# Whole float32 softmax parts for six half pairs, more transposes by DMA, float32 cluster similarities

## The chip, the core and the metric

One core of a Trainium2 chip runs the whole kernel. The metric is the device time of one execution in microseconds (us). The engines are TensorE (PE, its weight loads apart as PEld), VectorE (DVE), ScalarE (ACT), GpSimd (POOL) and SyncE (SP, which issues most DMAs). Each works through its own instructions in order and waits for others by semaphores.

## What is computed

A clustered attention and two feed-forward blocks. A query attends only to the keys whose nearest centroid is its own.

```python
B, H, S, D = 2, 8, 768, 64            # 16 heads in all, 16 centroids a head
q_assign = argmax(q_n @ c_n, axis=-1)  # normalised; the same for keys
mask = q_assign[:, :, :, None] == k_assign[:, :, None, :]
scores = where(mask, q @ k.T / sqrt(D), -1e9)
attn = exp(scores - max(scores)); attn /= sum(attn) + 1e-9
x = (attn @ v), heads side by side     # 1536 tokens x 512
h = x @ w_in;  x = elu(h) @ w_out      # 512 -> 2048 -> 512
out = ((x @ w_a) * (x @ w_b)) @ w_out2 # 512 -> 1536 -> 512
```

## The kernel before

Every step is a small function marked `@op`, and the string `ORDER` lists all steps as words such as `sc:3.4` (score tile 4 of head 3). The loop at the end calls them in that order; so each engine gets its instructions in the order of the words that use it, and tile pools add the waits. The 60 words `wm` are groups of eight bfloat16 products that go nowhere and stand between the early steps. An index after the last dot often names the engine (0 DVE, 1 ACT, 2 POOL).

Heads go in pairs, 8 pairs `j` of heads 2j and 2j+1; the 768 queries of a head are 6 tiles `t` of 128, in two halves `f` of three tiles.

- Loads: `lk` brings a head's transposed keys (64x768), `lq` its transposed queries twice, one copy under the other. `qa`, `qb`, `ka1`, `ka2`, `kb`/`kbd` split scaled queries and keys into a rounded part and its rest (`kbd` copies by DMA).
- Similarities: `sm` (two halves per pair) sums eight products of split centroids (`cst`, made by `c4`) with the split queries and keys, 64x384, in PSUM; `sv` copies them out; `st` transposes six blocks back to tokens by centroids (`tp`). `m1` to `m5` find the maximum's place and make a one-hot matrix, `oh`, `ohs`, `ohd` turn it and put it as 16 rows into `qb` and `kb`, so that the mask comes with the score product. For pair 0 `ot` and `oe` do this.
- Scores: `sc` makes a tile 128x768 in PSUM with four products (two buffers), `rm` takes its negative maximum on DVE, `ex` the exponential `pf` and its sum on ACT.
- Softmax parts for the value product need keys on partitions. Of the 96 tiles 66 go over PE: `tr` transposes three blocks of float32 `pf` into PSUM, `th` rounds them to float16 (first part), and `tl` on DVE subtracts that from PSUM to give the second part. Each is called twice per tile. The other 30 go by DMA: `hi` rounds `pf` to float16, `lo` on POOL subtracts to give the rest, and `td` issues one DMA transpose of both parts from SP's queue.
- Values: `vl` loads them into `acc`, `vs` scales them per head (`staged`), `v1` and `v2` split them into two float16 parts. `av` (three words per pair and half) adds six key blocks x three products of parts, for each of two heads, which write different halves of the output partitions.
- Scaling: `ra`, `rc` invert the sums, `rx` spreads them on POOL, `rb` turns them with three products with the identity, `re` copies them out and `ev` multiplies the value product by them into `acc`.
- Feed-forward weights come as 64-bit numbers in 68 pieces; `wl` loads a piece, `wa` to `wq` split it. The first pieces are made during attention.

Of the kernel before, what the change touches and what calls it, by code (L numbers as in the profile page):

```python
# [10 lines left out]
F32 = mybir.dt.float32  # L11
F32R = mybir.dt.float32r
F16 = mybir.dt.float16
# [28 lines left out]
NPHL = 3  # L42
# [35 lines left out]
rm:0.3 ex:1.2 wm:44 tl:1.0.1 w2:1 lq:5.0 tr:1.0.0 wm:12 th:1.0.0.1 v1:1.1 tr:1.1.0 th:1.1.0.1 sc:0.4
wm:9 tl:1.0.0 wm:36 rm:0.4 ra:0.0 ex:0.3 w3:1 w4:1 rc:0.0 tr:1.1.1 lk:4.0 th:1.1.1.1 sm:1.1 sc:0.5
hi:1.2.1 tl:1.1.1 ex:0.4 sv:1.1.1 wm:34 st:1 tl:1.1.0 rm:0.5 qa:4.1 wm:32 kbd:2 lo:1.2 ka1:4.2  # L80
v1:2.1 wh:1 ex:0.5 td:0.2 tr:0.3.0 sc:1.4 wm:35 rx:0.0 tr:0.3.1 sc:1.3 lk:5.0 th:0.3.0.1 m1:1
hi:0.5.1 m2:1 th:0.3.1.1 v2:1.2 v2:2.2 m3:1 m4:1 ka2:4.2 m5:1 tl:0.3.0 wm:43 oh:1 rm:1.3 ohs:1
tr:0.4.0 ex:1.3 tl:0.3.1 rm:1.4 ws:1 qb:4 th:0.4.0.1 td:1.2 av:0.0.0 rb:0.0 ohd:1 tr:0.4.1 sc:1.5
re:0.0.1 th:0.4.1.1 wl:2 tl:0.4.0 rm:1.5 tl:0.4.1 ex:1.4 qa:5.1 wq:1 tr:1.3.0 th:1.3.0.1 tr:1.3.1
av:0.0.1 th:1.3.1.0 tr:1.4.1 lq:7.0 ex:1.5 th:1.4.1.1 lo:0.5 ra:0.1 tl:1.3.1 sc:2.0 tl:1.3.0 rm:2.0
hi:1.5.1 tr:1.4.0 sc:2.1 ex:2.0 av:0.0.2 ka1:5.2 vs:4 lo:1.5 td:0.5 tl:1.4.1 rm:2.1 sc:2.2 tr:2.0.0
th:1.4.0.1 rc:0.1 tr:2.0.1 tl:1.4.0 ex:2.1 th:2.0.0.1 th:2.0.1.1 rx:0.1 lk:6.0 sc:3.0 rm:2.2 ex:2.2
rb:0.1 td:1.5 tl:2.0.0 tl:2.0.1 ka2:5.2 qb:5 rm:3.0 tr:2.1.1 ev:0.0 hi:2.2.2 sc:3.1 re:0.1.1
tr:2.1.0 wa:2 lo:2.2 sm:2.0 th:2.1.0.1 lq:6.0 ex:3.0 lk:7.0 sc:3.2 rm:3.1 sv:2.0.1 tr:3.0.0
th:2.1.1.1 ex:3.1 tl:2.1.0 w0:2 w1:2 sm:2.1 th:3.0.0.1 rm:3.2 tl:2.1.1 tl:3.0.0 ex:3.2 ra:1.0  # L90
tr:3.1.0 w2:2 sv:2.1.1 sc:2.3 rc:1.0 w3:2 th:3.1.0.1 tr:3.0.1 sc:2.4 av:0.1.0 rm:2.3 st:2 tl:3.1.0
th:3.0.1.1 rx:1.0 hi:3.2.1 ex:2.3 w4:2 tl:3.0.1 m1:2 m2:2 wh:2 tr:3.1.1 lo:3.2 rm:2.4 sc:2.5 wl:3
ws:2 m3:2 rm:2.5 v1:3.1 qa:6.1 rb:1.0 re:1.0.1 av:0.1.1 th:3.1.1.1 m4:2 ka1:6.2 av:0.1.2 m5:2
tl:3.1.1 ex:2.4 tr:2.3.0 sc:3.3 oh:2 tr:2.3.1 ex:2.5 ka2:6.2 th:2.3.0.1 td:3.2 wq:2 ohs:2 kbd:4
v2:3.2 sc:3.4 td:2.2 rm:3.3 tr:2.4.1 tl:2.3.0 ev:0.1 ex:3.3 hi:2.5.2 th:2.3.1.1 th:2.4.1.1 tr:2.4.0
rm:3.4 lo:2.5 sc:3.5 ex:3.4 th:2.4.0.1 tl:2.3.1 av:1.0.0 rm:3.5 av:1.0.1 wa:3 qa:7.1 av:1.0.2 ohd:2
ka1:7.1 ex:3.5 tl:2.4.1 qb:6 qb:7 ka2:7.2 sc:4.0 tr:3.3.0 tr:3.4.1 th:3.3.0.1 kbd:5 tl:2.4.0 sc:4.1
tr:3.3.1 hi:3.5.1 rm:4.0 tl:3.3.0 w0:3 th:3.4.1.1 rm:4.1 ex:4.0 lq:9.0 lo:3.5 tl:3.4.1 vs:5
th:3.3.1.1 ra:1.1 rc:1.1 ex:4.1 tl:3.3.1 w1:3 rx:1.1 sm:3.0 sc:4.2 tr:3.4.0 sv:3.0.1 tr:4.0.0 sc:5.0
th:3.4.0.1 rm:4.2 v1:4.2 rb:1.1 th:4.0.0.1 vs:7 tl:3.4.0 ex:4.2 re:1.1.1 tr:4.1.0 hi:4.2.1 sc:5.1  # L100
tl:4.0.0 tr:4.0.1 w2:3 sm:3.1 lo:4.2 vs:6 th:4.1.0.1 rm:5.0 th:4.0.1.1 lq:8.0 ex:5.0 v1:5.2 tl:4.1.0
# [1039 lines left out]
```

## Time and profile before

| | us |
|---|---|
| median of 3 runs | 818.26 (817.41 to 818.92) |
| profiled execution | 818.15 |
| its span, first to last instruction | 816.4 |

| engine | busy us of the span | instructions |
|---|---|---|
| PE | 807.5 | 4626 |
| DVE | 592.6 | 876 |
| ACT | 410.8 | 737 |
| POOL | 340.7 | 295 |

A group of instructions is shown with its line, engine, operation, out<-in, count, then busy time, mean duration of one in ns, and the idle time before them. Records of consecutive PE instructions overlap, since an instruction enters while the one before it drains; so a PE instruction is priced by how far apart the starts are, not by the mean duration.

### The profile page before, as it was taken

Reading aid. Unit: us, or ns where it says so; the run is one execution under the profiler, and the core shown is the slowest. Engines: PE = TensorE matmul, PEld = TensorE weight load, DVE = VectorE, ACT = ScalarE, POOL = GpSimd, SP = SyncE. Lnnn points to the kernel's source line nnn. Section 1 sums busy time; section 2 is a strip of 40 time slices with the busy share of each in tenths; the row PEclk is TensorE's granted clock in tenths of the full one; section 3 lists DMA queues with packets and bytes.
Section 4 is the critical chain, followed back from the end, with each engine's and each line's share of the span. In section 5 each row is a group of like instructions: output and inputs, shape, how many; then the busy total and the mean of one; then the engine's idle time right before and its main releaser. Section 6 shows DMA issues by size and latency. Waiting matters only on the chain.

```text
span 816.4 us, 12164 instructions
## 1 busy us (share of the span) xinstructions
PE 807.5 (99%) x4626; PEld 655.4 (80%) x4626; DVE 592.6 (73%) x876; ACT 410.8 (50%) x737; POOL 340.7 (42%) x295
## 2 busy tenths in 40 slices
PE   9999999999999999999999999999999999999998
PEld 8877777777777888888888888888888888888886
DVE  5889898999999757898778787875257874565222
ACT  7689878888896542643544464432122322232020
POOL 3576786587462233464444442341043441422000
PEclk9999999999999999999999999999999999999999
DMA  9446655565542202232222212122002221110102
GB/s 278 110 97 129 146 125 110 129 138 116 110 81 78 78 27 78 77 104 78 79 95 81 80 60 72 52 77 78 1 26 77 78 78 52 53 52 0 52 1 103
DMA packets 65626, 68.12 MB, mean 83 GB/s; under 512 B 49888, under 2 KB 49888, under 8 KB 65568
## 3 DMA queue, kind: packets, MB, share of 16 engines
q1 hardware_dynamic: 65328, 66.76, 30.6%
q8 instruction: 36, 0.59, 0.3%
q10 hardware_dynamic: 240, 0.59, 0.3%
q14 instruction: 22, 0.18, 0.1%
HBM read 48.27 MB, written 3.15 MB: 63 GB/s over the span
## 4 chain that ended last, share of the span: by engine, by line
PE 90%; POOL 5%; ACT 3%; issue 2%; DVE 0%; POOLq 0%; ACTq 0%
PE ab L927 8%; PE ab L925 8%; PE ab L926 8%; PE sc L673 6%; PE h L926 5%; PE h L925 5%; PE x L926 5%; PE x L925 5%; PE h L927 5%; PE x L927 5%; PE av L786 4%; PE o L927 4%; PE o L925 4%; PE o L926 4%; PE tt L727 4%; PE warm_ps L409 3%
## 5 line engine op out<-in xcount | busy, mean ns | idle before, releaser
L681 DVE TENSOR_REDUCE nm<-sc 128x1 f32<-128x768 f32 x96 | 90.8, 950 | 7.1 <-PE sc L673 6.0
L694 ACT ACTIVATE pf<-sc,nm 128x768 f32<-128x768 f32 x96 | 86.8, 905 | 15.7 <-POOL phl L709 6.9
L1027 ACT COPY t0ab<-ab 128x512 f32<-128x512 f32 x36 | 21.1, 587 | 108.5 <-PE ab L927 108.5
L736 DVE TENSOR_TENSOR pt<-tt,pt 128x384 f16<-128x384 f32 x132 | 70.0, 545 | 5.0 <-ACT pt L731 4.6
L1032 DVE TENSOR_TENSOR t1ab<-ab,t0ab 128x512 f32<-128x512 f32 x36 | 24.8, 688 | 63.2 <-ACT t0ab L1027 63.2
L727 PE MATMUL tt<-identf,pf 128*128 128x128 f32 x396 | 62.0, 277 | 1.4 <-ACT pf L694 1.4
L731 ACT CAST pt<-tt 128x384 f16<-128x384 f32 x122 | 55.9, 478 | 10.4 <-PE tt L727 9.8
L709 POOL TENSOR_TENSOR phl<-pf,phl 128x768 f16<-128x768 f32 x30 | 50.0, 1668 | 24.8 <-ACT phl L702 23.5
L673 PE MATMUL sc<-ka,qa 128*128 128x384 f32 x192 | 57.6, 381 | 2.5 <-ACT pf L694 2.4
L856 ACT ACTIVATE wg<-wraw 128x512 f32<-128x512 f32 x68 | 45.1, 667 | 25.5 <-DMA wraw<-in_w_out_dram 13.8
L727 PEld LDWEIGHTS tt<-identf,pf 128*128 128x128 f32 x396 | 46.0, 140 | 12.0 <-issue 4.3
L786 PE MATMUL av<-pt,v 128*64 128x384 f16 x576 | 52.7, 329 | 0.0
L873 DVE SCALAR_TENSOR_TENSOR wf<-wraw,wg 128x512 int32<-128x512 int32 x68 | 51.0, 751 | 1.8
L886 DVE SCALAR_TENSOR_TENSOR wg<-wraw,wg 128x512 f32<-128x512 uint32 x68 | 49.1, 723 | 1.7
L673 PE MATMUL sc<-kb,qb 80*128 80x384 f32 x192 | 49.6, 339 | 0.0
L1043 DVE TENSOR_TENSOR gl<-t1ab,gh 128x512 fp32r<-128x512 f32 x36 | 33.9, 941 | 18.7 <-ACT gh L1038 18.5
L861 DVE TENSOR_SCALAR wg<-wg 128x512 f32<-128x512 f32 x68 | 38.4, 566 | 8.8 <-ACT wg L856 8.6
L786 PEld LDWEIGHTS <-v 128*64 128x64 f16 x576 | 30.0, 109 | 18.4 <-issue 7.1
L866 DVE TENSOR_SCALAR wg<-wg 128x512 int32<-128x512 int32 x68 | 38.5, 567 | 1.8
L989 ACT CAST gh<-t1h 128x1024 fp32r<-128x1024 f32 x24 | 25.3, 1052 | 27.7 <-DVE t1h L981 27.7
L1083 DVE TENSOR_TENSOR acc<-o,acc 128x1024 f32<-128x1024 f32 (+1 forms) x12 | 14.2, 1180 | 32.3 <-PE o L927 32.3
L971 ACT ACTIVATE t0h<-h 128x1024 f32<-128x1024 f32 x24 | 24.6, 1024 | 23.3 <-PE h L927 23.2
(386 smaller groups left out, 2349.6 us busy)
## 6 DMA issues: line engine op xcount, KB each, us to landing
wraw<-in_w_out_dram SPq DMA_DIRECT2D x28, 512.0 KB, 3.3
wraw<-in_w_in_dram SPq DMA_DIRECT2D x16, 512.0 KB, 3.6
wraw<-in_w_a_dram SPq DMA_DIRECT2D x12, 512.0 KB, 3.5
wraw<-in_w_b_dram SPq DMA_DIRECT2D x12, 512.0 KB, 3.4
rawq<-in_qt_dram SPq DMA_DIRECT2D x30, 192.0 KB, 3.6
acc<-in_v_dram SPq DMA_DIRECT2D x4, 768.0 KB, 11.0
rawk<-in_kt_dram SPq DMA_DIRECT2D x15, 192.0 KB, 3.7
kb<-ka SPq DMA_DIRECT2D x14, 192.0 KB, 3.7
```

The lines of the kernel that those rows point to most:

```text
L673: nc.tensor.matmul(s[:, j, :HALF], a[:, qs], b[:, j * HALF : (j + 1) * HALF], start=i == 0, stop=i == 1,)
L681: nc.vector.reduce_max(out=nm, in_=st[g][f"sc{t}"][:, :, :HALF], axis=AX.XY, negate=True)
L694: nc.scalar.activation(pf.rearrange("p (a b) -> p a b", a=2), st[g].pop(f"sc{t}")[:, :, :HALF], AF.Exp, bias=st[g].pop(f"nm{t}"), accum_ou ...
L709: nc.gpsimd.tensor_sub(phl[:, S:], st[g].pop(f"pf{t}"), phl[:, :S])
L727: nc.tensor.transpose(tt[:, k * P : (k + 1) * P], pf[:, o : o + P], identf)
L731: (nc.vector.tensor_copy, nc.scalar.copy)[e](next(parts_of(g, t, u)), st[g][f"tt{t}{u}"])
L736: nc.vector.tensor_sub(lo, st[g].pop(f"tt{t}{u}"), hi)
L786: nc.tensor.matmul(pairs[j]["av"][x * 64 : (x + 1) * 64].rearrange("p (a q) -> p a q", a=3), st[2 * j + x][("v1", "v2")[vi]][:, kt_, :], s ...
L873: nc.vector.scalar_tensor_tensor(out=f, in0=raws[n][:, :, 1], scalar=-0x40000000, in1=g, op0=ALU.bitwise_and, op1=ALU.bitwise_or,)
L925: nc.tensor.matmul(ps, lhi, rhi, start=first, stop=False)
L926: nc.tensor.matmul(ps, lhi, rlo, start=False, stop=False)
L927: nc.tensor.matmul(ps, llo, rhi, start=False, stop=last)
```

## The change

- Similarities: `lk` loads the keys of both heads of a pair (128x768), a new `lp` does the same for queries, beside `lq`, which stays. `sm` is one step per pair: for each of six token blocks it multiplies the raw 128x128 block of queries, then of keys, as weights with 32 columns of normalised centroids (`cblk`, both heads' blocks) in plain float32, straight into `tp`. `sv` and `st` and the split centroids go. In odd heads the key parts now lie in swapped partition halves (`halves`).
- Whole parts: for the six (pair, half) in `WHOLE`, the first halves of pairs 0 to 5, `tr` works as before, `th` copies in float32 (no `tl`), and a new `aw` multiplies these with the unsplit `staged` values in float32. Of the other tiles, 54 go by `td` and six over PE with `tl`.
- `rb` uses transposes in place of products with the identity.
- Engines: `lo`, `qb`, `ka2` can run on DVE. Of 54 `lo` 19 stand on DVE and 35 on POOL; of 54 `hi` 38 on ACT; of 84 `th` 27 on DVE.
- `phl` has four buffers, not three, and a word in `ORDER` can name the buffer it takes. `ORDER` is another list throughout. `ce`, which loads the exponential's table early, moves to the end of attention.

Words that differ in number: `tr` and `th` 132 to 84, `tl` 132 to 12, `hi`, `lo`, `td` 30 to 54, `av` 48 to 30, `aw` 0 to 18, `sm` 16 to 8, `sv` 16 to 0, `st` 8 to 0, `lk` 16 to 8, `lp` 0 to 8.

```diff
-NPHL = 3
+NPHL = 4
+
+WHOLE = {(0, 0), (1, 0), (2, 0), (3, 0), (4, 0), (5, 0)}
...
     @op
-    def sm(j, hf):
...
-        for n, (a, b) in enumerate(prods):
-            nc.tensor.matmul(ps, a, b, start=n == 0, stop=n == len(prods) - 1)
...
+    def sm(j):
         tp = pairs[j]["tp"] = small([P, NT, 64], f"tp_{j}")
+        c = cblk[:, j % (H // 2)].rearrange("p x c -> p (x c)")
         for t in range(NT):
-            nc.tensor.transpose(
-                tp[:, t, :], pairs[j]["sim"][:, t * P : (t + 1) * P], identf[:64, :64]
-            )
+            for n, name in enumerate(("rawp", "rawk")):
+                nc.tensor.matmul(
+                    tp[:, t, 32 * n : 32 * n + 32], pairs[j][name][:, t * P : (t + 1) * P], c,
+                    start=True, stop=True,
+                )
...
     @op
-    def lo(g, t):
+    def lo(g, t, e):
         phl = st[g][f"phl{t}"]
-        nc.gpsimd.tensor_sub(phl[:, S:], st[g].pop(f"pf{t}"), phl[:, :S])
+        (nc.vector, None, nc.gpsimd)[e].tensor_sub(phl[:, S:], st[g].pop(f"pf{t}"), phl[:, :S])
 
     def pt_of(g, f):
         if f"pt{f}" not in st[g]:
-            st[g][f"pt{f}"] = take(ap, "pt", [P, 3, 2 * NT, P], F16, f"pt{f}_{g}", 4)
+            shape, dt = ([P, 3, NT, P], F32) if (g // 2, f) in WHOLE else ([P, 3, 2 * NT, P], F16)
+            st[g][f"pt{f}"] = take(ap, "pt", shape, dt, f"pt{f}_{g}", 4)
         return st[g][f"pt{f}"]
...
         for a in range(3):
-            nc.tensor.matmul(p[:, a, :], pairs[j]["rx", f][:, a, :], identf, start=True, stop=True)
+            nc.tensor.transpose(p[:, a, :], pairs[j]["rx", f][:, a, :], identf)
...
+    def aw(j, f, n):
+        if n == 0:
+            pairs[j]["av"] = take(psumA, "av", [P, HALF], F32, f"av_{j}_{f}")
+        for kt_ in (2 * n, 2 * n + 1):
+            for x in range(2):
+                g = 2 * j + x
+                nc.tensor.matmul(
+                    pairs[j]["av"][x * 64 : (x + 1) * 64].rearrange("p (a q) -> p a q", a=3),
+                    staged(g)[:, kt_ * D : (kt_ + 1) * D], st[g][f"pt{f}"][:, :, kt_, :],
+                    start=kt_ == 0, stop=kt_ == NT - 1,
+                )
```

## Rows read from the trace of the kernel before

**Rows 1.** The page: busy time in us, then tenths in 40 slices.

```profile
PE 807.5 (99%) x4626; PEld 655.4 (80%) x4626; DVE 592.6 (73%) x876; ACT 410.8 (50%) x737; POOL 340.7 (42%) x295
...
DVE  5889898999999757898778787875257874565222
...
PEclk9999999999999999999999999999999999999999
```

**Rows 2.** Stretches: length, busy PE, PEld, DVE, ACT, POOL, clock, DMA share, GB/s.

```profile
30.30:269.80 239.50, 235.42 (x1823) 180.07 (x1821) 219.93 (x367) 198.80 (x421) 149.36 (x135) 1.00 0.52 113
269.80:816.40 546.60, 542.94 (x2396) 449.23 (x2394) 355.28 (x472) 191.11 (x268) 177.56 (x122) 1.00 0.20 63
```

**Rows 3.** The chain in order of time: start us, us, engine, tile, line, count.

```profile
1.20 14.36 PE warm_ps L409 x216
...
124.50 1.82 PE sm L573 x8
126.32 0.91 PE sc L673 x4
127.23 0.99 PE tt L727 x9
...
128.92 0.82 PE rbp L767 x6
129.74 0.52 PE tp L587 x6
...
132.50 2.07 PE av L786 x24
```

**Rows 4.** Groups of DVE by form: `tl`, `th`, `re`; columns as on the page.

```profile
L736 DVE TENSOR_TENSOR pt<-tt,pt 128x384 f16<-128x384 f32 x132 | 70.0, 545 | 5.0 <-ACT pt L731 4.6
...
L731 DVE CAST pt<-tt 128x384 f16<-128x384 f32 x10 | 5.5, 548 | 2.3 <-PE tt L727 2.3
...
L772 DVE COPY rb<-rbp 128x384 f32<-128x384 f32 x4 | 2.2, 554 | 0.5 <-PE rbp L767 0.4
```

**Rows 5.** Groups of ACT by form: `th`, `hi`, `sv`, `ka1`.

```profile
L731 ACT CAST pt<-tt 128x384 f16<-128x384 f32 x122 | 55.9, 478 | 10.4 <-PE tt L727 9.8
...
L702 ACT CAST phl<-pf 128x768 f16<-128x768 f32 x12 | 10.0, 837 | 0.0
...
L579 ACT COPY sim<-sm 64x384 f32<-64x384 f32 x12 | 5.6, 464 | 1.3 <-PE sm L573 1.2
...
L523 ACT CAST ka<-rawk 64x768 fp32r<-64x768 f32 x6 | 4.9, 830 | 0.1
```

**Rows 6.** Single lines: subtractions in SBUF on DVE, shortest/median/longest ns, first and last start.

```profile
L944 DVE TENSOR_TENSOR x1l<-acc,x1h x4: 1211/1220/1227, 254.1 to 510.5; 128x1024 fp32r<-128x1024 f32 x4
...
L530 DVE TENSOR_TENSOR ka<-rawk,ka x1: 1946/1946/1946, 6.6 to 6.6; 64x768 fp32r<-64x768 f32 x1
...
L1043 DVE TENSOR_TENSOR gl<-t1ab,gh x36: 677/694/1781, 526.5 to 793.1; 128x512 fp32r<-128x512 f32 x36
```

**Rows 7.** DMA transposes: issues and landing; a pair of them on SP; stretches as in Rows 2.

```profile
L741 SPq DMA_TRANSPOSE pt<-phl x30: 1275/1440/2931, 42.1 to 241.7; - x30
...
DMA to landing us min/median/max: 3.6/3.8/5.5
...
92.02 3.71 SPq L741 DMA_TRANSPOSE pt<-phl  x2
...
60.00:240.00 180.00, 176.76 (x1336) 134.04 (x1337) 166.84 (x277) 155.89 (x338) 121.58 (x110) 1.00 0.58 123
94.00:98.00 4.00, 4.00 (x28) 3.49 (x27) 3.74 (x8) 3.77 (x11) 3.10 (x5) 1.00 1.09 196
98.00:100.00 2.00, 2.00 (x12) 1.35 (x12) 1.71 (x4) 2.00 (x5) 1.09 (x1) 1.00 0.18 71
```

**Rows 8.** Timeline: the first score product on PE; the exponential's table load on ACT.

```profile
30.35 0.60 PE L673 MATMUL sc<-ka,qa 128*128 128x384 f32 x2
...
9.72 1.28 ACT L346 ACT_TABLE_LOAD   x1
```

More of the change, by code (lines that the diff above doesn't have):

```diff
@@ L299, in clustered_attention_moe_kernel @@
     pools = {}
+    named, taken = {}, {}
     def take(pool, tag, shape, dt, name, bufs=1):
-        return pool.tile(shape, dt, tag=tag, bufs=bufs, name=name)
+        if bufs > 1:
+            n = taken[tag] = int(named.pop(tag, (taken.get(tag, -1) + 1) % bufs))
+            tag = f"{tag}_{n}"
+        return pool.tile(shape, dt, tag=tag, bufs=1, name=name)
     def small(shape, name, dt=F32):
@@ L355, in cz @@
     def cz(_):
-        for k in ("q1", "q2", "k1", "k2"):
-            nc.gpsimd.memset(cst[k].bitcast(F32), 0.0)
+        nc.gpsimd.memset(cblk, 0.0)
     @op
@@ L481, in flat, with minus_scaled @@
         return t.rearrange("p t d -> p (t d)")
-    def minus_scaled(out, a, scale, b):
-        nc.vector.scalar_tensor_tensor(
+    def minus_scaled(e, out, a, scale, b):
+        (nc.vector, None, nc.gpsimd)[e].scalar_tensor_tensor(
             out=out, in0=a, scalar=scale, in1=b, op0=ALU.mult, op1=ALU.subtract
@@ L503, in lk, with lp @@
     @op
-    def lk(g, e):
-        t = st[g]["rawk"] = take(ep, "rawk", [64, S], F32, f"rawk_{g}", 2)
-        (nc.sync, nc.scalar)[e].dma_start(out=t, in_=kt[g])
+    def lk(j, e):
+        t = pairs[j]["rawk"] = take(ep, "rawk", [P, S], F32, f"rawk_{j}", 2)
+        (nc.sync, nc.scalar)[e].dma_start(out=t, in_=kt[2 * j : 2 * j + 2].rearrange("x d s -> (x d) s"))
+    @op
+    def lp(j, e):
+        t = pairs[j]["rawp"] = take(ep, "rawp", [P, S], F32, f"rawp_{j}", 2)
+        (nc.sync, nc.scalar)[e].dma_start(out=t, in_=qt[2 * j : 2 * j + 2].rearrange("x d s -> (x d) s"))
     @op
@@ L519, in operand, with halves @@
         return st[g][name]
+    def halves(g):
+        x = 64 * (g % 2)
+        return slice(x, x + 64), slice(64 - x, P - x)
     @op
     def ka1(g, e):
+        a, _ = halves(g)
         (nc.vector.tensor_copy, nc.scalar.copy, nc.gpsimd.tensor_copy)[e](
-            operand(g, "ka")[0:64], st[g]["rawk"]
+            operand(g, "ka")[a], pairs[g // 2]["rawk"][a]
         )
@@ L528, in ka2 @@
     def ka2(g, e):
-        k = operand(g, "ka")
-        (nc.vector, None, nc.gpsimd)[e].tensor_sub(k[64:P], st[g]["rawk"], k[0:64].bitcast(F32))
+        k, (a, b) = operand(g, "ka"), halves(g)
+        (nc.vector, None, nc.gpsimd)[e].tensor_sub(
+            k[b], pairs[g // 2]["rawk"][a], k[a].bitcast(F32)
+        )
     @op
     def kb(g):
-        nc.scalar.copy(operand(g, "kb")[0:64], st[g]["rawk"])
+        nc.scalar.copy(operand(g, "kb")[0:64], pairs[g // 2]["rawk"][halves(g)[0]])
     @op
@@ L538, in kbd @@
         nc.sync.dma_start(
-            out=operand(g, "kb")[0:64].bitcast(F32), in_=operand(g, "ka")[0:64].bitcast(F32)
+            out=operand(g, "kb")[0:64].bitcast(F32),
+            in_=operand(g, "ka")[halves(g)[0]].bitcast(F32),
         )
@@ L717, in parts_of @@
         f, a = divmod(t, 3)
-        return (pt_of(g, f)[:, a, i * NT + 3 * u : i * NT + 3 * (u + 1)].rearrange("p m q -> p (m q)")
-                for i in range(2))
+        parts = 1 if (g // 2, f) in WHOLE else 2
+        return [pt_of(g, f)[:, a, i * NT + 3 * u : i * NT + 3 * (u + 1)].rearrange("p m q -> p (m q)")
+                for i in range(parts)]
     @op
@@ L1092, in ob @@
         send(a, t)
-    for word in ORDER.split():
+    for line in ORDER.split():
+        word, *buffers = line.split("/")
+        named.update(n.split("=") for n in buffers)
         name, args = word.split(":")
```

443 lines of the change are left out of this document (218 added, 225 removed).

## The prediction

> **What bounds the kernel now.** I read the page first, then stretches of busy time, then the chain of waits in order of time, then single lines. [rows 1] TensorE (PE) is busy for 807.5 of 816.4 us, at the full granted clock in all forty slices. A busy PE alone proves little, so the reader looks at the two stretches of [rows 2]: from the first score product (30.35 us [rows 8]) to the last scaling of attention (269.8 us) PE is busy for 235.4 of 239.5 us, VectorE (DVE) for 219.9 (92%), ScalarE (ACT) for 198.8 (83%), GpSimd (POOL) for 149.4. Behind that, in the feed-forward part, PE is full again and the others have room. [rows 3] shows the same as a chain: from 124.50 to 134.57 us nearly every piece is PE, one behind the other. So time is what PE has to do, and an edit is worth its PE time so long as DVE, ACT and the DMAs keep up, and DVE has 20 us to spare in the stretch, no more.
>
> **PE, part by part**, priced by the contiguous pieces of [rows 3]. A similarity product costs 1.82/8 = 0.228 us, a transpose of a similarity block 0.52/6 = 0.087, a softmax transpose 0.99/9 = 0.110, an instruction of the float32 product that spreads the reciprocals 0.82/6 = 0.137 (three products, six records: a float32 product is two instructions), a value product in float16 2.07/24 = 0.086, a warm-up product in bfloat16 14.36/216 = 0.066.
>
> *Similarities.* Gone: 8 pairs x 16 products = 128 x 0.228 = 29.2 us, and 48 transposes x 0.087 = 4.2. Added: 8 x 12 float32 products = 192 instructions that load 128 weight columns and pass only 32. No row has this form. The nearest is the transpose of a similarity block (float32, 128 weight columns, 64 passed): 0.087. From above the reciprocal's 0.137 (128 passed) bounds it, from below the warm-up's 0.066. I take 0.075, under the nearest row since half as many columns pass: 14.4 us (12.7 to 26.3). Net -19.0 (-7 to -21).
>
> A page speaks against this. The Trainium skill, "TensorE: Matmul & The Clock Gate", LDWEIGHTS (loading the stationary operand), counts 1/1.2 ns per weight column whatever the rows, 107 ns for 128. By it the 192 instructions would take an estimated 20.5 us and the kernel would end about 6 us later than my sum. The trace disagrees: the similarity transposes load 128 columns each and follow each other at 87 ns [rows 3].
>
> *Reciprocals.* 96 instructions x 0.137 = 13.1 become 48 transposes x 0.110 = 5.3: -7.8.
>
> *Softmax transposes.* 132 groups of three become 84: 144 x 0.110 = -15.8. (36 tiles of the whole halves and 6 of the last pair stay on PE; 54 instead of 30 go by DMA.)
>
> *Value products.* Six halves lose 36 float16 products each: 216 x 0.086 = -18.6. They get 12 float32 products each, 144 instructions of 384 columns. Here I chose. Two float16 products into different output halves run side by side: 0.086 each, where a score product of the same 384 columns takes 0.91/4 = 0.228. A float32 instruction takes twice a bfloat16 one of the same shape (0.137 against 0.066). If float32 pairs run side by side too, one costs 2 x 0.086 = 0.172, in all 24.8 us; if not, twice that, 49.5. Both instructions of one product write the same half, so only every second neighbour can overlap, which in a row of them still keeps both halves busy. I take 24.8: net +6.2 (end: +31).
>
> Sum: -19.0 - 7.8 - 15.8 + 6.2 = -36.4 us of PE work. Warm-ups are as many as before (60 groups), so nothing is bought there. Some 3 us of it fall ahead of the first score product (one pair's similarities shrink and three groups of warm-ups move behind it); the stretch would shrink from 239.5 to about 206.
>
> **Who must keep up in 206 us.** *DVE* [rows 4, 6]: 120 of 132 subtractions go (70.0/132 = 0.530): -63.6; three similarity evictions (0.55, as the other copies from PSUM) -1.6; 17 more casts from PSUM (0.55) +9.4; four more evictions of reciprocals (0.55) +2.2; six small operations on the values' scale move behind the first score product, +2.4. New are 19 subtractions of 128x768 in SBUF and four more of 64x768. 1024 elements a partition take 1.21 us undisturbed, so 768 take 0.91; but the one 64x768 that DVE did took 1.95, with POOL at work, and the 128x512 ones spread from 0.68 to 1.78. I take 1.2 each, +27.6 (0.91 to 1.95: 21 to 45). DVE: 219.9 - 23.6 = 196. *ACT* [rows 5]: 65 casts less (55.9/122 = 0.458) -29.8, 12 similarity evictions less (5.6/12 = 0.47) -5.6, 4 reciprocal evictions less -1.9; 26 more float16 casts (0.83) +21.7, 5 key casts (0.82) +4.1. One table load of 1.28 [rows 8] no longer sits behind the warm-ups but in front of the first exponential. Some 189. *POOL* loses more key work than it gains in subtractions and stays near 146; I cost that at nothing, covered by a third of the stretch free.
>
> So DVE would be wanted for 196 of 206 us, 95%. An in-order engine is not on time at that share: I let the stretch grow until DVE is back at the 92% at which PE ran without gaps before, 196/0.92 = 213. That gives back 7 us. ACT then stands at 89%, up from 83.
>
> *DMA and SP's queue* [rows 7]. Before, the DMA engines were 58% busy from 60 to 240 us: 104 us. Two transposes behind each other (92.02) filled the engines at 1.09 for about 4 us, so one is worth at most 2.2. 24 more are 52 us, the queries' second load (3.1 MB; 123 GB/s at 58% is 212 at full) 15. That makes 171 us of 1.09-wide engine time in some 170 us: about 92% full. SP issues them in order at 1.44 each, 78 us for 54; key and query loads, copies of keys and one-hot rows stand behind a transpose that waits for its subtraction, and PE's next scores and value products wait for those. I put no time of its own on this, since the pieces overlap DVE's lag, but it is the thinnest cover.
>
> **Result of the likeliest case.** Profiled execution 818.15 us, 1.75 of it around the span, 0.1 below the median of 818.26. 818.15 - 36.4 + 7 = 789 (780 to 797 with 0.066 to 0.1 for a similarity instruction and 0 to 14 us of lag).
>
> **Rivals.** *B: float32 value products don't run side by side.* 24.8 more on PE; the others then have room again and the lag goes: 818.15 - 36.4 + 24.8 = 806 (801 to 809). For it: no row shows a float32 pair; against: the float16 pair.
>
> *C: DVE or the transposes set the pace.* If each of the 23 SBUF subtractions costs 1.95, DVE has 213 us to do and at 92% the stretch is 232: 7 us gained there, 3 ahead of it, 808; with a share of 95%, 224, 800. Full DMA engines (171 us at 92% of their 1.09, in bursts) end in the same place. So 798 to 812. For it: the long ones of [rows 6]; against: most of these operations are short ones.
>
> The page for this is the Trainium skill, "SBUF — State Buffer", SBUF: two separate sides: a VectorE operation with two SBUF inputs and a GpSimd operation shut each other out for a whole instruction. The trace agrees in part: of 128x512 subtractions the median is 694 ns, the longest 1781 [rows 6].
>
> *D: slower: transposes one at a time.* If a transpose must land (3.8 us) before the next moves, 54 of them take 205. They start near 55 us and the last was followed by 28 us of work (241.7 to 269.8): 55 + 205 + 28 = 288, 18 us later than before, 836. It decides from (269.8 - 28 - 55)/54 = 3.5 us a transpose. Against it: the two at 92.02 are issued within 3.71 us and done by 98, where the DMA share falls to 0.18.
>
> *E: no change*, savings all eaten by lag: 818.
>
> **How the numbers follow.** Forecast 0.55, B 0.14, C 0.17, D 0.07, E 0.03, and 0.04 for under 779 (no lag at all, similarities at the low end). The range 778 to 811 holds the first three, about 0.84, and takes in the bounds of the similarity and the value products. Faster by over 0.2% (what a measurement tells from no change, 1.6 us): 0.55 + 0.14 + 0.17 + 0.04 = 0.90; within 0.03; slower 0.07.
>
> **What would show it.** Similarity instructions closer than 0.09 us; value products in float32 near 0.17 us an instruction (0.34 is B); last scaling near 240 us instead of 269.8 with PE pieces still filling the chain; DVE near 92% of that stretch, its SBUF subtractions between 0.91 and 1.3 us (1.9 is C); SP's transposes issued near 1.5 us, DMA share under 1. The feed-forward part should keep its 546.6 us to within 2. I am wrong if PE shows idle time of more than some 15 us in the stretch, or if the feed-forward part starts short of weights.

## The result and the profile after

The changed kernel takes 811.24 us (810.02 to 812.25) beside 817.84 us for the kernel before on the same chip: 0.9917 of it, interval 0.9899 to 0.9935, a gain of 6.6 us. The forecast of 789 was a gain of 29, and 811.24 lies just above the upper end of 811. The profiled execution took 810.02 us, its span is 808.2. A trace shows one execution, here the shortest of four, so differences between traces can be some us off those between medians.

The page (busy time, tenths in 40 slices; against [rows 1]):

```profile
PE 789.1 (98%) x4378; PEld 642.4 (79%) x4378; DVE 576.4 (71%) x792; ACT 405.4 (50%) x689; POOL 339.1 (42%) x284
...
DVE  4899888889888867898777697875257873565222
...
PEclk9999998999899999999999999999999999999999
DMA  9558994989991212223222321122011221110102
```

Stretches, columns as in [rows 2]: first score product to last scaling, the feed-forward part, and two pieces of the first; under them the last piece in the kernel before:

```profile
28.40:260.50 232.10, 218.97 (x1580) 166.82 (x1578) 206.20 (x291) 192.44 (x374) 154.21 (x131) 0.97 0.80 165
260.50:808.20 547.70, 544.11 (x2400) 450.18 (x2399) 357.34 (x473) 192.93 (x270) 177.72 (x122) 1.00 0.20 63
...
130.00:165.00 35.00, 34.31 (x249) 24.97 (x248) 31.66 (x45) 31.15 (x60) 26.68 (x23) 1.00 0.78 157
...
195.00:245.00 50.00, 42.32 (x289) 29.06 (x286) 44.44 (x60) 42.20 (x81) 30.40 (x26) 0.93 1.04 190
```

```profile
195.00:245.00 50.00, 49.47 (x389) 38.57 (x388) 47.31 (x78) 44.40 (x99) 30.11 (x27) 1.00 0.48 91
```

Against [rows 2] the stretch shrank from 239.5 to 232.1 us, where 206 to 213 were forecast; the feed-forward part kept its time (547.7 against 546.6). PE is now idle for 13.1 us of the stretch (4.1 before) and its clock is down to 0.97 of full. From 195 to 245 us it is idle for 7.7 us (0.5 before) while DVE and ACT are at 89 and 84%: PE doesn't bound that piece any more.

The time between the start of one PE instruction and the start of the next, summed by kind over the attention's instructions (worked out from the two traces), shows where the sum went:

```
us on PE by kind                       before   after   change  forecast
similarities (products, transposes)     36.25   21.50   -14.75    -19.0
reciprocals                             11.49    6.89    -4.60     -7.8
softmax transposes                      42.59   31.70   -10.89    -15.8
value products                          51.66   62.60   +10.94     +6.2
score products                          79.20   88.67    +9.47      0
warm-ups, one-hot rows, others          34.66   36.42    +1.76      0
sum                                    255.85  247.78    -8.1     -36.4
of it: beyond 300 ns to the next start    4.1    20.3   +16.2
of it: the rest (PE's own pace)         251.7   227.5   -24.2
```

So the 28 us that are missing from PE's sum are of two kinds: 12 in its own pace, and 16 of waits, of which the forecast had allowed 7. PE's own pace also holds what its lower clock costs. Of the 20.3 us of waits 11.0 stand ahead of score products, which take a score buffer that the exponential must leave. What the weight load of score products waits for, before and then after (line, releaser, us, times, longest):

```profile
PEld sc L673 <- ACT pf L694: 5.6, 11, 1.1
```

```profile
PEld sc L683 <- ACT pf L704: 18.7, 30, 1.9
```

When they arise is seen in the starts of the score products, tile by tile (96 tiles in order of time; us from the span's start, worked out from the traces; the columns from "half tr." on are experiments below):

```
tile      before   after  half tr.  6 buf.  no lo   least   lo twice
0          30.35   28.35   28.14    28.14   28.24   28.02    28.12
16         67.55   64.82   64.54    63.92   62.99   63.42    66.44
40        127.97  114.81  114.11   113.52  112.52  112.31   121.91
44        135.83  130.09  128.20   124.45  122.46  122.25   133.10
64        179.18  173.05  171.12   168.22  164.39  164.08   178.14
80        218.56  208.47  205.72   203.30  198.96  196.95   223.91
95        249.70  239.02  237.06   234.76  228.30  226.34   263.62
last sc.  270.43  261.12  259.12   256.87  250.37  248.12   285.71
```

("last sc." is the end of the last scaling.) After has a lead of 13.2 us at tile 40, which is near the pace of the forecast. It loses 7.4 of it within four tiles, and ends with 9.3. Of the 7.4 us 2.1 are work that its order has there: "least" takes 9.94 us for these four tiles with PE never waiting and at full clock, before took 7.86. The other 5.3 us are waits (2.5) and a slower pace at a mean clock of 0.78. The four tiles stand in the chain of waits (start us, us, engine, tile, line; the first row is the same work elsewhere):

```profile
66.11 2.60 PE tp L596 x24
...
112.10 1.44 PE av L812 x8
...
114.53 3.28 DVE qb L502
...
118.33 3.44 PE tp L596 x24
```

on GpSimd and PE at that place (timeline):

```profile
114.43 1.78 POOL L519 TENSOR_TENSOR v<-acc,v 128x384 f16<-128x384 f32 x2
116.18 0.82 POOL L509 TENSOR_TENSOR acc<-acc,vsc 128x384 f32<-128x384 f32 x1
...
118.33 0.41 PE L596 MATMUL tp<-cblk,rawp 128*128 128x32 f32 x2 [1.91 <-DVE pt L743]
```

and the stretch behind it, with the clock:

```profile
120.00:124.00 4.00, 4.00 (x21) 3.90 (x21) 1.93 (x5) 2.38 (x6) 3.51 (x2) 0.55 0.28 86
```

A `qb` operation of DVE takes 3.28 us at 114.53; the same operation took 0.94 at its shortest in this kernel and 1.12 at its longest before. It ends 0.81 us after the last of three GpSimd operations that ran meanwhile, nearly the whole of its own shortest time. PE waits 1.91 us behind it, its clock then stands at 0.55 for four us, most of them at the lower of its two levels (1.2 rather than 2.4 GHz), and 24 similarity instructions take 3.44 us, where the 24 at 66.11 took 2.60.

### The profile page after: what moved, and what is told of

Its sections match the earlier page's. It is cut to its first block, busy times and chain, and to the rows that moved or that the text cites. A ratio compares the mean times of both kernels' runs of the same rounds, so it can differ in the third digit from the quotient of the medians.

```text
span 808.2 us, 11612 instructions
## 1 busy us (share of the span) xinstructions
PE 789.1 (98%) x4378; PEld 642.4 (79%) x4378; DVE 576.4 (71%) x792; ACT 405.4 (50%) x689; POOL 339.1 (42%) x284
## 4 chain that ended last, share of the span: by engine, by line
PE 83%; DMA 5%; DVE 5%; ACT 4%; issue 2%; POOL 1%; SPq 0%; ACTq 0%; DVEq 0%; POOLq 0%
PE ab L951 8%; PE ab L952 8%; PE ab L950 8%; PE h L950 5%; PE h L952 5%; PE x L950 5%; PE x L952 5%; PE h L951 5%; PE x L951 5%; PE sc L683 5%; PE o L951 4%; PE o L952 4%; PE o L950 4%; PE av L798 3%; DMA pt<-phl 2%; PE tt L739 2%
## 5 line engine op out<-in xcount | busy, mean ns | idle before, releaser
L691 DVE TENSOR_REDUCE nm<-sc 128x1 f32<-128x768 f32 x96 | 90.6, 951 | 14.4 <-PE sc L683 13.4
L719 POOL TENSOR_TENSOR phl<-pf,phl 128x768 f16<-128x768 f32 x35 | 60.3, 1725 | 28.1 <-ACT phl L712 25.5
L1057 DVE TENSOR_TENSOR t1ab<-ab,t0ab 128x512 f32<-128x512 f32 x36 | 24.8, 689 | 63.2 <-ACT t0ab L1052 63.2
L683 PE MATMUL sc<-ka,qa 128*128 128x384 f32 x192 | 59.6, 392 | 8.5 <-ACT pf L704 7.3
L881 ACT ACTIVATE wg<-wraw 128x512 f32<-128x512 f32 x68 | 45.3, 672 | 24.8 <-DMA wraw<-in_w_out_dram 15.3
L898 DVE SCALAR_TENSOR_TENSOR wf<-wraw,wg 128x512 int32<-128x512 int32 x68 | 52.7, 775 | 1.8
L683 PEld LDWEIGHTS sc<-ka,qa 128*128 128x128 f32 x192 | 30.1, 196 | 23.3 <-ACT pf L704 18.7
L739 PE MATMUL tt<-identf,pf 128*128 128x128 f32 x252 | 40.6, 283 | 1.0 <-ACT pf L704 0.8
L1021 DVE TENSOR_TENSOR gl<-t1h,gh 128x1024 fp32r<-128x1024 f32 x24 | 31.9, 1331 | 8.7 <-ACT gh L1014 8.7
L739 PEld LDWEIGHTS tt<-identf,pf 128*128 128x128 f32 x252 | 30.6, 145 | 8.3 <-ACT pf L704 3.6
L1006 DVE SCALAR_TENSOR_TENSOR t1h<-t0h,h 128x1024 f32<-128x1024 f32 x24 | 29.1, 1216 | 10.6 <-ACT t0h L1001 10.6
L683 PEld LDWEIGHTS sc<-kb,qb 80*128 80x128 f32 x192 | 36.2, 195 | 0.0
```

The costliest lines, as they stand in the source:

```text
L683: nc.tensor.matmul(s[:, j, :HALF], a[:, qs], b[:, j * HALF : (j + 1) * HALF], start=i == 0, stop=i == 1,)
L691: nc.vector.reduce_max(out=nm, in_=st[g][f"sc{t}"][:, :, :HALF], axis=AX.XY, negate=True)
L719: (nc.vector, None, nc.gpsimd)[e].tensor_sub(phl[:, S:], st[g].pop(f"pf{t}"), phl[:, :S])
L739: nc.tensor.transpose(tt[:, k * P : (k + 1) * P], pf[:, o : o + P], identf)
L881: nc.scalar.activation(wgf[n][0].bitcast(F32), raws[n][:, :, 1].bitcast(F32), AF.Abs)
L898: nc.vector.scalar_tensor_tensor(out=f, in0=raws[n][:, :, 1], scalar=-0x40000000, in1=g, op0=ALU.bitwise_and, op1=ALU.bitwise_or,)
```

## Experiments

Four theories were set against each other at first. Theory 1: the DMA engines are full. Theory 2: four buffers for softmax parts are too few, so casts wait for transposes. Theory 3: DVE's operations on two SBUF inputs and GpSimd's shut each other out. Theory 4: it is PE's own work, similarity instructions above all. A fifth came from the first runs.

**Half of each transpose.**

```
-        nc.sync.dma_start_transpose(out=pt_of(g, f)[:, a], in_=...)
+        nc.sync.dma_start_transpose(out=pt_of(g, f)[:, a, :NT], in_=...[:, :S])
...
-                    st[2 * j + x][f"pt{f}"][:, :, pi * NT + kt_, :],
+                    st[2 * j + x][f"pt{f}"][:, :, kt_, :],
```

> The changed kernel, but each of the 54 DMA transposes moves only the first float16 part (768 of 1536 columns), and the value products read that part where they should read the second; so the second part of the softmax is left out there. Nothing else moves. Theory 1 (the DMA engines are full: share 1.08 from 195 to 243 us, and PE waits behind it): the share there falls under 0.8, PE's idle time in attention from about 18 us to under 8, and the time from 811 to 790-798. Theory 2 (four phl buffers are too few, whatever the engines carry): also faster, since a buffer comes free earlier, so this run alone does not part 1 from 2. Theory 3 (VectorE and GpSimd shut each other out of SBUF, one qb took 3.28 us): unchanged within 3 us. Theory 4 (PE's own work, similarities at 0.112 us an instruction instead of 0.075): unchanged within 3 us.

806.26 us (805.54 to 808.04). From 195 to 245 us:

```profile
195.00:245.00 50.00, 43.43 (x285) 29.96 (x282) 43.67 (x59) 41.98 (x80) 29.81 (x25) 0.90 0.51 101
```

The DMA share halves, from 1.04 to 0.51, and PE, DVE and ACT hardly notice. In the table of tiles, from tile 44 to the end the kernel takes 130.9 us, after 131.0. So full DMA engines do not set the pace there. Theory 1 had expected 790 to 798 and theories 3 and 4 at most 3 us; the gain of 5 us fits none of them. Between the two traces it is 2.0 us, of which 1.9 came in ahead of tile 44; where the other 3 arose no trace shows.

**Six buffers for the parts.** The names of buffers in the order go with it.

```
-NPHL = 4
+NPHL = 6
```

> The changed kernel with six phl buffers in place of four, taken in turn. Theory 1: ScalarE no longer stands in front of a buffer, but the transposes land no earlier; the wait moves to the value products; DMA share from 195 to 243 us stays above 1.0; 807 to 812. Theory 2: the waits of ScalarE and GpSimd for a transpose's landing go and with them 10 us or more: 795 to 802. Theories 3 and 4: 811 within 2.

807.90 us (805.75 to 808.47), ratio to before 0.9866 (0.9851 to 0.9881). This version computes everything, and is faster than both kernels, but theory 2 had expected 795 to 802. Its stretch at the place where after lost its lead:

```profile
120.00:124.00 4.00, 4.00 (x37) 3.04 (x34) 3.96 (x6) 3.21 (x8) 2.94 (x3) 1.00 0.42 130
```

The wait ahead of the similarities is 0.72 us rather than 1.91 and the clock stays up. That holds for the profiled execution, the shortest of the four (805.75 us at a mean clock of 0.996); the others took some 2 us more at 0.991 to 0.992. From tile 44 on it is no faster than after (132.4 us).

**Both at once** (the two diffs above).

> Half transposes (second softmax part not used) and six buffers for the parts together. Theory 1 with theory 2 (full DMA engines and too few buffers each hold the stretch up by themselves): the gains of 5 and 3 us add up, 802 to 804. If neither sets the pace and what both took away is one and the same wait: 805 to 808, as either alone.

808.18 us (806.10 to 809.32): the gains do not add up, as if both had taken away one and the same wait. That it is the one around tile 40 the traces do not settle: PE waited 0.73 us at that place here, and 0.74 with half transposes alone, and the clock fell in both all the same (half transposes first):

```profile
120.00:124.00 4.00, 4.00 (x17) 3.90 (x17) 2.56 (x4) 2.30 (x5) 1.71 (x1) 0.50 0.27 86
```

```profile
120.00:124.00 4.00, 4.00 (x18) 3.90 (x19) 1.37 (x4) 1.94 (x4) 3.07 (x2) 0.50 0.07 19
```

**Pair 6's first half whole too** (48 transposes by DMA). In the order the names of the `phl` buffers go, and `pt` buffers get other names.

```
-WHOLE = {..., (5, 0)}
+WHOLE = {..., (5, 0), (6, 0)}
```

> The changed kernel with pair 6's first half as a seventh whole half: six DMA transposes less (48), 12 groups of PE transposes more (3.9 us at 0.11) and 24 instructions of float32 value products for 36 of float16 (0.8 us more). Theory 1: the DMA engines are relieved by about 12 us in the stretch where they are fullest; 801 to 808. Theory 2: about the same as theory 1, as buffers are asked for less often. Theories 3 and 4: PE's 4.7 us more are paid: 813 to 817.

829.88 us (824.00 to 831.71). A transpose now lies on the chain with 4.56 us at 179.58, another with 4.13 at 62.80, and PE is idle for 6.1 and 4.7 us around them. Both lie ahead of the first new step, which stands behind 75 of the 96 score tiles. Up to there only the buffers differ, 36 words for `phl` and 14 for `pt`, and yet tile 64 starts at 193.33 us rather than 173.05 (from the traces). So the run tells nothing of a seventh whole half. It shows that the choice among these buffers alone can cost some 20 us: the wait that theory 2 names can be large, though six buffers took away little of it in after.

**Before with the new similarities and reciprocals alone.** The steps stand in the order of before, `sm` in the place of `st`.

```
-WHOLE = {(0, 0), ..., (5, 0)}
+WHOLE = set()
```

> The kernel before with two parts of the change alone: the float32 similarities straight from raw keys and queries, and the reciprocals by transposes. No whole halves, 30 DMA transposes, the order of before with these steps in the places of the old ones. PE loses 36.2 - 21.5 = 14.7 us on similarities (at the 0.112 seen) and 6.3 on reciprocals, 21 in all. Theories 1 and 2: the transposes do not stand in the way here, so most comes through until VectorE's 218 us of work fill the shorter stretch: 800 to 807. Theory 4 says the same. Theory 3: the float32 subtractions stay on GpSimd; the same. If these parts bring under 5 us, the loss is not with the transposes at all.

835.03 us (833.51 to 841.47): 17 us slower than before, though the two kinds took PE 31.0 us rather than 47.7 (28.4 in after; from the traces). The 24 similarity instructions now stand in one block where 16 and 6 had stood apart, and the engines wait for what PE does behind them:

```profile
ACT pt L730 <- PE tt L726: 23.4, 21, 5.8
ACT pf L691 <- PE tt L726: 10.4, 5, 4.5
```

As a price of the two parts it is of no use, since parts, order and buffers (its words name `tt` buffers, those of before none) can't be told apart in it. It does show that PE work taken out of an order made for other work need not be time saved.

**Theory 5**, from these: PE's work shrank, and where only halves of the old kind are left (their parts made by ACT, DVE and GpSimd, 54 transposes in place of 30) these engines, each in order, DVE and ACT at 89 and 84%, set the pace of score product, maximum, exponential, next score product.

**No second part on DVE** (on top of half transposes; the second part of softmax is used nowhere).

```
-        (nc.vector, None, nc.gpsimd)[e].tensor_sub(phl[:, S:], st[g].pop(f"pf{t}"), phl[:, :S])
...
+        if e:
+            nc.gpsimd.tensor_sub(phl[:, S:], pf, phl[:, :S])
```

> The kernel with half transposes (806.3), and VectorE's 19 subtractions that make the second softmax part (0.95 to 1.1 us each) are left out as well; the second part is nowhere used here, in either kernel. Theory 5 (in the stretch from 195 to 243 us, where only halves of the old kind are left, VectorE and ScalarE, about 90% busy and in order, set the pace of score product, maximum and exponential, and TensorE stands idle for 8 us): nine of the 19 lie there, so that stretch loses 5 to 9 us and the kernel takes 797 to 802. Theory 4 (TensorE's own work is the bound): 805 to 808.

802.46 us (802.34 to 806.57), 3.8 less than with half transposes alone. From 195 to 245 us:

```profile
195.00:245.00 50.00, 44.95 (x306) 32.36 (x305) 37.60 (x55) 42.36 (x81) 29.16 (x25) 0.97 0.55 111
```

**Nor on GpSimd.** The two lines with a plus above go as well.

> As the kernel without VectorE's subtractions of the second softmax part, with GpSimd's 35 (60 us) left out too. Theory 3 (VectorE's operations on two SBUF inputs wait for GpSimd's: qb up to 3.28 us where 0.94 is usual, some 16 us of VectorE over the shortest times): most of the stretched operations shrink and the time falls another 4 to 8 us under that kernel, to 790 to 797. Theory 5: within 2 us of that kernel, since GpSimd had a third of the stretch free. Theory 4: 805 to 808.

798.77 us (797.96 to 799.71), 3.7 less again, though GpSimd had seemed free for a third of the stretch. Theory 5 alone had expected under 2. So GpSimd's subtractions (1.7 us each) were in the way too. That they keep DVE out (theory 3) is at most a small part of it, since DVE's operations hardly shrink; here are the 14 `qb`, with GpSimd's subtractions and without:

```profile
L502 DVE SCALAR_TENSOR_TENSOR qb<-rawq,qa 64x768 fp32r<-64x768 f32 x14 | 18.0, 1287 | 0.7 <-ACT qa L577 0.7
```

```profile
L502 DVE SCALAR_TENSOR_TENSOR qb<-rawq,qa 64x768 fp32r<-64x768 f32 x14 | 17.1, 1224 | 0.7 <-ACT qa L577 0.7
```

That leaves what waits for GpSimd: with its subtractions ACT's exponentials waited 1.3 us for them and SP 2.6, and what that is worth no run isolates.

**Moved rather than left out.** Six buffers and DVE's subtractions on GpSimd; then six buffers with the subtractions back on DVE, and ACT's casts ahead of them on GpSimd. In the order (one step of 19, one of 15):

```
-lo:0.3.0
+lo:0.3.2
```

```
-hi:3.3.1
+hi:3.3.2
```

> Six buffers, and all 19 of VectorE's subtractions of the second part given to GpSimd (1.65 us each there: GpSimd 150 to about 180 of 230 us). Theory 5: VectorE gains 19 us, the kernel takes 800 to 805 against 807.9 with six buffers alone. Theory 3 (the two engines shut each other out): no gain or a loss, 807 to 814, since GpSimd's operations get longer and stand in the way of what is left on VectorE.

> Six buffers, and the 15 float16 casts of softmax parts that stand on ScalarE ahead of a VectorE subtraction given to GpSimd (0.82 us each on either). Theory 5 (ScalarE and VectorE, in order, set the pace late in the stretch): ScalarE has some 12 us less to do, and the kernel takes 802 to 806 against 807.9 with six buffers alone. Theory 3 (VectorE and GpSimd shut each other out): the casts stand ahead of the subtractions that wait for them, 808 to 812. Theory 4 (TensorE's own work): within 1 us of 807.9.

810.36 us (808.89 to 812.85) and 814.96 us (812.02 to 818.17), both slower than six buffers alone (807.90). GpSimd is now the full one, in the first (195 to 245 us, DVE 37.73, GpSimd 45.86):

```profile
195.00:245.00 50.00, 41.32 (x288) 27.84 (x285) 37.73 (x50) 41.93 (x82) 45.86 (x35) 0.97 1.03 189
```

The first number is what theory 3 had expected (807 to 814), but `qb` took no longer than with six buffers alone (18.1 us, 18.0), so DVE was not kept out more. In these two moves a lighter DVE or ACT was not worth what GpSimd then held up.

**Half a maximum.** Six buffers; the maximum leaves out the second half of the keys.

```
-            out=nm, in_=st[g][f"sc{t}"][:, :, :HALF], axis=AX.XY, negate=True
+            out=nm, in_=st[g][f"sc{t}"][:, 0, :HALF], axis=AX.X, negate=True
```

> Six buffers, and the maximum of each row of scores taken over the first half of its keys alone (the second half is left out of the maximum): 0.95 us becomes some 0.55 for 96 tiles. It takes 38 us from VectorE and 0.4 us from each round score product, maximum, exponential. Theory 5: TensorE's waits for the exponential (18 us) fall by half or more, 796 to 802 against 807.9. Theory 4: 806 to 808.

801.48 us (801.07 to 805.92), 6.4 less than six buffers alone. PE's wait for the exponential falls; with six buffers, then here:

```profile
PEld sc L679 <- ACT pf L700: 18.4, 32, 1.9
```

```profile
PEld sc L679 <- ACT pf L700: 11.3, 21, 1.2
```

That is what theory 5 had expected, with nothing on PE touched. The edit takes some 38 us off DVE and 0.4 us off each round at once, so DVE's load and the length of the round are not told apart.

**Double the suspect.** Six buffers, and each of DVE's 19 subtractions done twice.

```
-        (nc.vector, None, nc.gpsimd)[e].tensor_sub(phl[:, S:], st[g].pop(f"pf{t}"), phl[:, :S])
...
+        for _ in range(1 if e else 2):
+            (nc.vector, None, nc.gpsimd)[e].tensor_sub(phl[:, S:], st[g][f"pf{t}"], phl[:, :S])
```

> Six buffers, and each of VectorE's 19 subtractions done twice: 19 us more for VectorE and nothing else. Taking these away gave 4 us (802.5 against 806.3), a fifth of their time. Theory 5: at least as much is lost again, 811 to 818 against 807.9. If VectorE's load is beside the point: 807 to 809.

834.64 us (830.54 to 836.94): 26.7 us lost for 25.9 us more on DVE (its subtractions take 47.3 us against 21.4 with six buffers). From 195 to 245 us:

```profile
195.00:245.00 50.00, 39.16 (x198) 27.64 (x197) 44.67 (x49) 32.13 (x58) 23.70 (x18) 0.74 0.77 139
```

More than foreseen. DVE was at its limit: what was added there was paid in full, 20 us of it in waits of PE and the rest in a slower pace at the lower clock (0.74 here); what was taken away gave back a fifth (3.8 us for some 20). How much of the loss is DVE's load, and how much that each transpose gets its part later, the run doesn't part.

**What is left without them.** Six buffers, half transposes, no subtraction on either engine, half a maximum: "least" in the table of tiles.

> Six buffers, no subtraction for the second softmax part on either engine (the second part isn't used, its half of each transpose is left out), and the maximum over half of the keys: what is left is TensorE's work and a VectorE with some 57 us less. If TensorE's sum of the forecast stands but for the similarity instructions (0.112 us rather than 0.075, 192 x 0.037 = 7 us), its bound without any lag is 818.15 - 36.4 + 7 = 789: theory 5 in full (all that is over this is lag behind VectorE and GpSimd) says 789 to 794. If there is another lag, or TensorE's other terms were sized wrong, it stays at 796 or more.

794.92 us (792.80 to 797.93). The four lie in pairs, 792.80 and 792.85 us at a mean clock of 1.00, 796.99 and 797.93 at 0.993; the profile is of 796.99. Stretches, and PE's longest wait:

```profile
28.00:248.10 220.10, 214.14 (x1584) 164.89 (x1582) 145.74 (x274) 191.92 (x374) 91.47 (x96) 0.98 0.55 125
248.10:795.20 547.10, 543.48 (x2398) 449.70 (x2396) 356.81 (x473) 192.30 (x270) 177.73 (x122) 1.00 0.20 63
```

```profile
PEld sc L679 <- ACT pf L700: 12.0, 19, 1.4
```

By kinds as in the first table, PE's sum here is 234.75 us, of it 11.3 beyond 300 ns and 223.4 at its own pace: 28.3 less than before, where the forecast's sum with the measured similarity instructions says 36.4 - 7.1 = 29.3. So PE's sum was right to 1 us but for that term. Of the 8 us that this execution is over 789, 7.2 are waits more than before; 5.6 of its 11.3 us of waits lie from 189 to 223 us, where the chain now runs over ACT's exponentials and casts. The two executions at full clock are 4 us over 789.

**The forecast's other terms.** Heads of a value product one behind the other:

```
...
-        for kt_ in (2 * n, 2 * n + 1):
-            for x in range(2):
+        for x in range(2):
+            for kt_ in (2 * n, 2 * n + 1):
```

> The changed kernel with the float32 value products of the two heads one behind the other (four products of one head, then four of the other) rather than in turn. If neighbours in different output halves run side by side, as the 0.161 us from start to start suggests, the 144 instructions go to 0.3 us or more where they stand in a row of one half: up to 20 us of TensorE more, 816 to 830. If 0.161 us is what one costs by itself: no change, 810 to 813.

811.13 us (809.71 to 811.53): no change. Six of the instructions, in after and here (timeline):

```profile
112.03 1.19 PE L812 MATMUL av<-pt,acc 128*64 128x384 f32 x6
```

```profile
58.01 1.20 PE L812 MATMUL av<-pt,acc 128*64 128x384 f32 x6
```

So 0.16 us is what such an instruction costs on average, whichever half the product beside it writes. In both runs the two instructions of one product start within 0.014 us of each other, and the next product 0.31 to 0.32 us later (from the traces). Similarities with 64 columns passed rather than 32 for the queries (a neighbour's columns, overwritten behind it):

```
...
-                    tp[:, t, 32 * n : 32 * n + 32], pairs[j][name][:, t * P : (t + 1) * P], c,
+            nc.tensor.matmul(tp[:, t, :], pairs[j]["rawp"][:, block], wide, start=True, stop=True)
...
```

> The changed kernel with 64 columns passed rather than 32 in the similarity instructions of the queries (half of the 192, and 12 more of them). If the 128 weight columns set the 0.112 us from start to start, that stays and the time is that of the changed kernel, 809 to 813. If the passed columns count (as the first forecast of 0.075, half the way under the 0.087 of transposes, had it), these go to 0.14 us or more and the kernel takes 3 us longer, 813 to 816.

812.50 us (811.37 to 816.10): no change that the spread lets one tell. In the chain, two wide and two narrow instructions by turns:

```profile
65.81 0.25 PE tp L598 x2
66.06 0.20 PE tp L601 x2
66.26 0.25 PE tp L598 x2
```

Two wide and two narrow take 0.45 us, 0.112 each, much as narrow ones alone did (2.60/24 = 0.108): what the wide ones take longer, the narrow ones behind them make up. Whether 32 or 64 columns pass doesn't count here; that the load does is read from the forms with 128 and 64 rows, below.

**Feed-forward casts later in the order** (six buffers).

```
-... cE:0 re:5.1.0/rb=1 ... xh:0.0 ... xl:0.0 ... xh:0.1 ... xl:0.1
+... rm:15.4 xh:0.0 xl:0.0 ... rm:15.5 xh:0.1 xl:0.1
```

> Six buffers, and the first chunk's two casts on ScalarE (1.04 us each) and two subtractions on VectorE (1.22 us each) for the feed-forward part moved in the order from about 215 us, where scores wait for them, to about 235 us behind the last maxima. Theory 5: TensorE's waits near 215 to 222 us shrink by 2 to 4 us, 804 to 806. If the feed-forward part then starts later, the gain is given back: 808 to 810.

808.91 us (806.81 to 810.83): no gain over six buffers. The trace shows a gain that is given back, as the second expectation had it. The last score tile starts at 232.69 us rather than 234.76; then PE waits behind two of the moved operations (the chain, and the timeline of PE, here and with six buffers):

```profile
232.86 0.96 ACT x0h L960
233.84 0.97 DVE x0l L965
```

```profile
235.59 1.83 PE L735 MATMUL tt<-identf,pf 128*128 128x128 f32 x9 [1.94 <-DVE rb L780]
```

```profile
235.79 1.48 PE L735 MATMUL tt<-identf,pf 128*128 128x128 f32 x9
```

The nine transposes start where they did, and take longer; the clock is at 0.57 from 236 to 240 us. So these operations do hold scores up, by some 2 us, and moving them only moved the wait.

## Why the prediction failed

**Similarities: the step that mis-sized a term.** It took 0.075 us an instruction, under the transposes of a similarity block, "since half as many columns pass". It is 0.108 to 0.112 (the chain above), so 192 cost 21.5 us rather than 14.4: 7.1 us. The nearest row in [rows 3] was another one: the softmax transposes load 128 x 128 weights in float32, as these do, and take 0.110. The similarity transposes load only 64 rows (form 64\*128 in the trace). The Trainium skill, "TensorE: Matmul & The Clock Gate", LDWEIGHTS (loading the stationary operand), counts 1/1.2 ns per weight column, by which the estimate was 107 ns for 128 and a kernel some 6 us later. The trace of after agrees on the price; I had held the 0.087 of another form against it. The page also counts columns whatever the rows, and that the transposes with 64 rows and 128 columns don't bear out: at 0.087 they are closer than 107 ns.

**Value products: right size, wrong reason.** 144 instructions take 22.1 us at their own pace (0.153 each; 24.8 forecast at 0.172). But float32 products don't need a neighbour in the other half for it, as heads in a row showed: it is the two instructions of one product whose starts lie together, and I had taken them to be the ones that can't overlap. That the size came out is luck. Rival B rested on the same wrong reading, and its 24.8 us could not have come.

**Softmax transposes** were sized right. In after they gave 4.9 us less than forecast because PE ran part of what is left at the lower clock and with waits between: with the waits gone ("least") 252 transposes take 26.5 us, 0.105 each. **Reciprocals** gave 3.2 less, and half of that was a wrong price: the 96 instructions of before took 11.5 us in all, 0.120 each, and not the 0.137 of the six in [rows 3].

**The lag: the step that failed most.** I shared DVE's 196 us out over the whole stretch, let it grow until DVE was back at 92%, and put down 7 us. Two things were wrong. First, an average over the stretch hid its last third. Tile 64 to the last scaling's end, before and after (columns as in [rows 2]):

```profile
179.18:270.43 91.25, 90.72 (x681) 69.82 (x680) 85.03 (x143) 73.56 (x154) 47.50 (x43) 1.00 0.41 88
```

```profile
173.05:261.12 88.07, 80.00 (x542) 58.31 (x541) 77.38 (x113) 70.49 (x135) 51.99 (x44) 0.96 0.88 168
```

There PE's own pace falls from 90.8 to 78.0 us (from the traces) and DVE's busy time from 85.0 to 77.4: DVE would have had to be busy for 99% of what PE needs (94 before). Up to tile 64 it is 129.5 of 135.6, 95% (93). So the last third comes out only 3.2 us shorter, with 10.1 us of waits where there had been 0.7. Second, and this is argued rather than shown, 92% on DVE without gaps was a property of the order of before, where PE had work to put between one score product and the next. With less of that work PE waits for the same round. Measured, where 7 us had been put down: 16.2 us more of waits, and beside them (1 - 0.97) x 232.1 = 7.0 us of PE's full pace lost to the clock, which before stood at 1.00 and of which the forecast had nothing; part of the 7.0 lies within the waits. What the runs say of it: the two subtraction sets 3.8 and 3.7 us, half of each maximum 6.4 (measured by itself, on six buffers), the DMA and buffer wait 3 to 5, not additive. With all of these gone ("least") 16 of the 22 us over 789 went, and PE's work was not touched.

**DVE's subtractions** took 1.16 us on average (19 of them, 21.9 us; 1.2 forecast), right. What was not in the sum is that other DVE operations get longer. `qb` (14 in the stretch):

```profile
L502 DVE SCALAR_TENSOR_TENSOR qb<-rawq,qa 64x768 fp32r<-64x768 f32 x14 | 19.1, 1361 | 0.0
```

```profile
L484 DVE SCALAR_TENSOR_TENSOR qb<-rawq,qa 64x768 fp32r<-64x768 f32 x14 | 13.3, 955 | 1.5 <-ACT qa L545 1.5
```

After first, then before: 5.8 us more for the same work, and part of why DVE was busy for 206 us of the stretch and not for 196. The Trainium skill, "SBUF — State Buffer", SBUF: two separate sides, says that such an operation and one of GpSimd that reads SBUF shut each other out for a whole instruction. The 3.28 us at 114.53 agree with it. The loss when subtractions move to GpSimd is no sign of it, since `qb` got no longer there.

**GpSimd** was put at nothing, at 146 us and with a third of the stretch free. It was busy for 154.2, and leaving its subtractions out gave 3.7 us: room on average did not mean in time.

**DMA: the thinnest cover held.** A transpose takes 1.66 us to issue at the median of 54 (1.44 in [rows 7]), and the DMA share passes 1 from 195 to 245 us, as feared. Yet half the bytes change nothing there. D (one transpose at a time) is out: SP issued six within 11.7 us from 226.74, where D needs 3.5 for each. E was close in time, and its reason, lag, holds for two thirds: of what PE's own pace gave, 16.2 of 24.2 us went into waits.

**Signs and range.** Faster was right, and so were the subtractions' price and the feed-forward part (547.7 us). Similarity instructions (0.108 for under 0.09), the last scaling (260.5 for 240) and the DMA share (1.04 from 195 to 245 us) gave the miss away. The sign that I had named for being wrong, over 15 us idle on PE, did not show: its records leave 13.1 idle, while the waits from start to start are 20.3. The range ended at C's 811, since C was priced on DVE's load alone and as if PE's similarity term could not miss at the same time. That C's stretch of 232 us is the measured one is luck: C had DVE at 213 us and 92%, and it was at 206 and 89%. A sum was off too: 0.1 for a similarity instruction and 14 us of lag give 801, not 797.

**What stays open.** Why the clock fell at waits of 0.73 and 0.74 us and not at one of 0.72; what the last 4 us between "least" at full clock and 789 are made of, beyond ACT being on the chain in the profiled execution; what DVE's load and the length of the round are worth apart; and what each part of the change is worth alone, since the run for it mixed parts, order and buffers.

## What to carry to other kernels

When work is taken off the engine that bounds a kernel, price the lag by stage: in each, set what every other engine has to do beside what is left for the bounding one, not its share of the whole stretch. Here an in-order engine at 89% was at its limit: 26 us more on it cost 27, and 20 less gave back 4. Where little passes, choose the nearest row for an instruction by what it loads and by its type, and only then by what it passes. And an edit that changes which buffers steps take is an experiment on buffers, whatever else it changes.

## What was not expected of the hardware

A float32 product of 64 weight columns and 384 passed ones costs 0.16 us for each of its two instructions, beside the same half or the other, while float16 ones take 0.086 [rows 3]. A DVE operation on two SBUF inputs took 3.28 us for 0.94 beside three GpSimd operations. PE's clock went to its lower level after waits of 0.73 to 1.91 us in the same place in three kernels of four (0.55, 0.50 and 0.50 from 120 to 124 us; 1.00 with six buffers), while in the kernel before waits of up to 1.08 us were followed by no fall. After one of these falls 24 similarity instructions took 0.84 us longer.
